# Attention of the later batches in 13 stretches of TensorE's time instead of 15, and a new written order of the other engines

## The chip, the cores and the metric

The kernel runs on one core of a Trainium2 chip. The metric is the time of one execution on the device in microseconds (us), the median of three runs. The core's engines run side by side, each through its own queue of instructions in a fixed order: TensorE (PE in the profile) multiplies, VectorE (DVE), ScalarE (ACT) and GpSimd (POOL) do everything else, and SyncE (SP) issues the transfers between memory and the on-chip buffer.

## What is computed

Chunked window attention over 4 batches of 8 heads, 768 positions and 64 columns, and behind it a mixture of 4 experts with 1024 hidden columns, in which every expert sees every token:

```python
# attention, for each chunk of 32 positions (window: 16 before, 8 after, and 8 memory keys)
scores = scale * q_c @ k_full.T
a = softmax(scores)
out[chunk] = a @ v_full
# experts, x = the attention's output as (3072, 512)
p = domain_probs / domain_probs.sum(-1)
for e in range(4):
    h = relu(x @ w1[e])           # (512, 1024)
    out += p[:, e:e+1] * (h @ w2[e])   # (1024, 512)
```

All of it is fp32. The large products are done in pairs of a rounded high part and the remainder (`_hi`, `_lo`), three matmuls for one, and by a scheme of seven block products instead of eight.

## The kernel before

**Stages.** The attention of one batch is cut into 8 units of 96 positions, 32 units in all. The first 60 us do batch 0's attention and its first expert. Then MID (n = 1 to 3, about 62 to 298 us) does the other experts of batch 0; it also makes the combinations of weights that the seven products need and stores them in memory. FIN (n = 4 to 15, about 298 us to the end) does batches 1 to 3, four experts each, with the weights streamed back in.

**Stretches.** The attention of the later units (8 to 31) is done between products of TensorE, in *stretches*: `window_of_two(us, vs)` puts the score matmuls of the units `us` (line 736) and the mixing matmuls, weights by values, of the units `vs` (line 758) onto TensorE one after the other. The softmax of the units scored in one stretch (a maximum on VectorE, the exponentials on ScalarE, a division and the transposes on VectorE) is done while TensorE goes on with the experts, and its result is mixed in the next stretch. The table `BY_TWO` says which units each stretch scores and mixes; its key is the step n and a place in it ("m" after the second pair of hidden columns, "A" after the last pair, "B" near the end). There are 15 stretches. The queries and keys of a unit are loaded ahead of its scores (`want_qk`) into one of a few places: a tile of their own (`qk_t`, in FIN for every second unit `qk_u`), or, in MID, a spare half of `xr` for the units in `SPARE`.

**The seven products.** In a step with pair p, the products of activations with the combined weights (line 999) come in the order one, two, six, five, seven of the pair and four and three of the pair before. Each leaves a result in `a_ps` or `moe_ps`, a few banks in turn, which ScalarE copies out (line 603) or VectorE adds up (line 621); then a relu (line 605), the multiplication with the routing weight (line 1101, `weigh`, or line 622 on GpSimd), a cast to the high part (`A_hi`, line 603) and the subtraction that leaves the remainder (`A_lo`, line 621 on VectorE or 622 on GpSimd). `Sa` and `Sb` are sums of such parts, `us` the steps of these sums. In MID the same engines also make the weights: `raw`, `s_t` and `raw_pair` are fp32 weights and their sums, `w` the parts for TensorE.

**What sets the order.** A list of operations is made in the order of the code; TensorE's own order follows it. For the other engines a written table, `MID_ORDER` or `FIN_ORDER`, names every operation by its number in base 36; an apostrophe means that it runs on the other engine that can do it (VectorE or GpSimd, ScalarE or VectorE). `follow` issues them in that order, and each engine then runs its queue strictly in that order, waiting for what its next instruction reads.

Of the kernel before, what the change touches and what calls it, by code (L numbers as in the profile page):

```python
# [18 lines left out]
P = 128  # L19
B, H, S, D = 4, 8, 768, 64  # L20
# [44 lines left out]
5k 67 5h 5p 7i 8u 5i 7p 6b 5m 7j 5s 6t 48 5q 5n 5u 8y 5r 5t 49' 7k 5o 7m 5w 5v 60 6e 7n 6m 4e 5x 6w 8v 61 6n 5y 6y 6f'
9m 62 7q 6x 7o 7t 4f 72 6v 5z 6s 8z 6u 7w 75 73 63 83 7u 77 81 6z 76 74 70 90 79 82 78 7x 7d 7v 7r a0 71 86 7s' 89 7z
91 7e 92 7y 7f 8w 8b 88 8a 7a 87 4a 84 8f 7b 9o 8c 9n 8i 7c 8d 8x 8g 7g 8k 4g a2 8j 80 8m 4h 96 8l 85 8h 99 4i 8q 94
4c 4j c9 ae 4b 4k 9e af 8r 4l ag 8s 4d ah 4m 9p ai 8n 9s aj 9q 4n 8o 8e 9u ak 9t 8p an 9v al 9r' am ar ao cb 8t ap ca
au at aq 9w cn 9f 97' as 9x 9a bx 9y a1 98' ax by 9b 9j 9c ay 9z bz 93 9d' 9h 95 c0 c1 cg cd' 9g c2 cl az ce c3 9i ch
# [1783 lines left out]
```

## Time and profile before

| | us |
|---|---|
| median of three runs | 1020.97 (1020.47 to 1021.89) |
| the profiled execution | 1021.78 |
| its span, first to last instruction | 1020.0 |
| TensorE busy in the span | 1011.6 (99%) |
| VectorE, GpSimd, ScalarE busy | 789.2 (77%), 544.5 (53%), 518.6 (51%) |

The granted clock of TensorE is 0.998 of full over the span. Read the table with the wait lists in mind: an engine that is 77% busy over the whole span can still be the one for which TensorE waits at one place.

### The profile page before, as it was taken

To read this page: it belongs to the slowest core of one execution; us is meant where nothing else is said; L and a number is where in the kernel's file an instruction comes from. 1 tells how busy PE (TensorE), PEld (TensorE's weight loads), DVE (VectorE), ACT (ScalarE), POOL (GpSimd) and SP (SyncE) were. 2 spreads that over 40 slices of the span, in tenths; PEclk is the share of its full clock that TensorE was granted. 3 is DMA by queue.
4 is the path that set the end of the run, shared out by engine and by line. 5 is a ranking of instruction groups with operands and counts; after the bars stand their busy time and mean duration, and the time that the engine had idled before them with its cause. 6 is when DMAs were issued, how large, how long until landed. Compare 5 with 4: busy or idle time off the path is not lost.

```text
span 1020.0 us, 20660 instructions
## 1 busy us (share of the span) xinstructions
PE 1011.6 (99%) x7566; PEld 975.3 (96%) x7566; DVE 789.2 (77%) x1245; ACT 518.6 (51%) x1415; POOL 544.5 (53%) x478
## 2 busy tenths in 40 slices
PE   8999999999999999999999999999999999999998
PEld 6898989989899999999999999999999999999998
DVE  5685987988969869797899759678697756849385
ACT  3756755747546465445655554453544535343241
POOL 4654733555559454586465714354276655527263
PEclk9999999999999999999999999999999999999999
DMA  8869989979789899899998987888778887878784
GB/s 274 293 210 363 362 324 390 382 286 382 282 288 354 292 377 312 301 367 313 353 291 280 287 269 252 287 267 276 236 253 277 293 263 257 271 246 278 248 257 146
DMA packets 184644, 299.28 MB, mean 293 GB/s; under 512 B 11904, under 2 KB 126176, under 8 KB 184544
## 3 DMA queue, kind: packets, MB, share of 16 engines
q1 hardware_dynamic: 184544, 297.97, 85.4%
q8 instruction: 60, 0.98, 0.4%
q14 instruction: 40, 0.33, 0.1%
HBM read 228.66 MB, written 69.26 MB: 292 GB/s over the span
## 4 chain that ended last, share of the span: by engine, by line
PE 98%; DVE 1%; issue 0%; ACT 0%; POOL 0%; DVEq 0%; POOLq 0%
PE a_ps L999 24%; PE a_ps L1289 20%; PE moe_ps L999 18%; PE moe_ps L1289 15%; PE moe_ps L978 13%; PE moe_ps L931 3%; PE s_ps L736 1%; PE x_ps L758 1%; PE moe_ps L758 1%; PE x_ps L1385 1%; PE att_ps L531 0%; DVE u L1101 0%; PE att_ps L1520 0%; PE att_ps L1476 0%; PE x_ps L1565 0%
## 5 line engine op out<-in xcount | busy, mean ns | idle before, releaser
L978 PE MATMUL moe_ps<-w,h_hi 128*128 128x512 f32 x384 | 119.4, 392 | 0.0
L603 ACT CAST A_hi<-u 128x384 fp32r<-128x384 f32 x144 | 72.8, 515 | 59.0 <-DVE u L1101 42.0
L603 ACT COPY u<-a_ps 128x384 f32<-128x384 f32 x120 | 57.2, 476 | 87.2 <-PE a_ps L999 86.8
L622 POOL TENSOR_TENSOR A_lo<-u,A_hi 128x384 fp32r<-128x384 f32 x47 | 53.1, 1133 | 83.5 <-ACT A_hi L603 83.5
L621 DVE TENSOR_TENSOR u<-moe_ps,u 128x384 f32<-128x384 f32 x120 | 66.1, 551 | 40.4 <-PE moe_ps L999 28.2
L999 PE MATMUL a_ps<-xc_hi,w 128*128 128x384 f32 x432 | 92.3, 334 | 0.0
L621 DVE TENSOR_TENSOR A_lo<-u,A_hi 128x384 fp32r<-128x384 f32 x97 | 84.5, 879 | 9.7 <-ACT A_hi L603 9.2
L978 PEld LDWEIGHTS moe_ps<-w,h_hi 128*128 128x128 f32 x384 | 71.3, 188 | 15.0
L622 POOL TENSOR_TENSOR u<-u,routes 128x384 f32<-128x384 f32 x43 | 45.3, 1056 | 75.4 <-ACT u L605 75.3
L1289 PE MATMUL a_ps<-A_hi,w 128*128 128x384 f32 x320 | 81.6, 335 | 0.1
L999 PEld LDWEIGHTS a_ps<-xc_hi,w 128*128 128x128 f32 x432 | 76.5, 188 | 0.5
L978 PE MATMUL moe_ps<-w,h_lo 128*128 128x512 f32 x192 | 75.0, 390 | 0.0
L621 DVE TENSOR_TENSOR acc<-a_ps,acc 128x384 f32<-128x384 f32 x78 | 42.9, 550 | 37.5 <-PE a_ps L1289 36.9
L1101 DVE SCALAR_TENSOR_TENSOR u<-u,routes 128x384 f32<-128x384 f32 x72 | 64.9, 911 | 0.2
L622 POOL TENSOR_TENSOR raw<-raw 128x256 f32<-128x256 f32 x41 | 37.2, 908 | 51.1 <-DVE raw L621 34.8
L621 DVE TENSOR_TENSOR u<-a_ps,u 128x384 f32<-128x384 f32 x60 | 33.1, 552 | 32.6 <-PE a_ps L999 27.3
L1289 PEld LDWEIGHTS a_ps<-A_hi,w 128*128 128x128 f32 x320 | 57.6, 188 | 0.8 <-DVE u L1101 0.6
L605 ACT ACTIVATE u<-u 128x384 f32<-128x384 f32 x72 | 37.9, 527 | 39.1 <-DVE u L621 38.6
L693 ACT ACTIVATE s_pair<-s_ps,mx_two 96x64 f32<-96x64 f32 x192 | 57.4, 322 | 0.3
L622 POOL TENSOR_TENSOR us<-u,us 128x384 f32<-128x384 f32 x33 | 41.3, 1252 | 26.1 <-DVE us L621 25.6
L999 PE MATMUL a_ps<-xc_lo,w 128*128 128x384 f32 x216 | 54.9, 334 | 0.0
L1289 PE MATMUL a_ps<-A_lo,w 128*128 128x384 f32 x160 | 53.5, 334 | 0.0
(254 smaller groups left out, 3068.8 us busy)
## 6 DMA issues: line engine op xcount, KB each, us to landing
w<-k SPq DMA_DIRECT2D x126, 512.0 KB, 4.6
w<-w SPq DMA_DIRECT2D x96, 512.0 KB, 5.5
w<-t SPq DMA_DIRECT2D x84, 512.0 KB, 6.0
k<-w SPq DMA_DIRECT2D x48, 512.0 KB, 5.9
raw<-in_w_dram SPq DMA_DIRECT2D x62, 256.0 KB, 5.2
w<-k SPq DMA_DIRECT2D x38, 256.0 KB, 4.5
raw_pair<-in_w_dram SPq DMA_DIRECT2D x32, 256.0 KB, 5.4
t<-t_hi SPq DMA_DIRECT2D x32, 256.0 KB, 5.6
```

What stands on the lines that cost most here:

```text
L603: nc.scalar.copy(out(), x())
L605: nc.scalar.activation(out(), x(), func)
L621: ("DVE", t_dve(cols), lambda: nc.vector.tensor_tensor(out=out(), in0=x(), in1=y(), op=op)),
L622: ("POOL", t_pool(cols), lambda: nc.gpsimd.tensor_tensor(out=out(), in0=x(), in1=y(), op=op)),
L693: now["plan"].add("ACT", t_act(KW) + 0.147, lambda i=i, h=h, j=j, g=g: nc.scalar.activation(whole()[:, i * H + h, :], at()[0:UQ, j, i, g, ...
L736: nc.tensor.matmul(at()[c * CH:(c + 1) * CH, j, i, g, :], lhsT=x[rows, g * UQ + c * CH:g * UQ + (c + 1) * CH], rhs=x[rows, k0:k0 + KW], st ...
L758: nc.tensor.matmul(out[j * D:(j + 1) * D, g, :], lhsT=late_st[w]["v"].ap[:, h * D:(h + 1) * D], rhs=late_st[w]["aT"][:, j * NPAIR + g, :], ...
L931: nc.tensor.matmul(ps.ap[:, lo:hi], lhsT=a[:, c * P:(c + 1) * P], rhs=x[:, c, lo:hi], start=(i == 0), stop=(i == len(steps) - 1),)
L978: nc.tensor.matmul(self.ps.ap, lhsT=h.ap[:, self.rows], rhs=w.ap[:, part, :], start=(i == 0 and k == 0), stop=(i == NF - 1 and k == 2),)
L999: nc.tensor.matmul(ps.ap[:, 0:SG], lhsT=a()[:, c * P:(c + 1) * P], rhs=y[:, k0 + c, :], start=(first and i == 0), stop=(i == len(steps) - ...
L1101: dve(lambda: nc.vector.scalar_tensor_tensor(out=u.ap, in0=x(), scalar=0.0, in1=r.ap, op0=ALU.max, op1=ALU.mult), SG, [r], [u] + keys, two ...
L1289: nc.tensor.matmul(ps.ap[:, 0:SG], lhsT=w_ap[:, y, rows], rhs=x.ap, start=(begins and k == 0 and i == 0), stop=(k == NP2 - 1 and i == 2), ...
```

## The change

Two stretches go: the one of step 3 in the middle of it ("m": scores of unit 15, mix of unit 14) and the one of step 7 ("m": scores of 23, mix of 21 and 22). Their units are put into the neighbouring stretches, which now score two units and mix two each. Unit 15's queries and keys are loaded into the spare half of `xr`, and those of unit 17, which would need a second tile, into a tile of `raw_pair` (the pool of the raw weight pairs, two places), after the last pair of step 3. No matmul is added or taken away; beside the stretches TensorE's order differs in four matmuls alone, the high part of the first product of pair (4, 0), which stand earlier, near the end of MID. Both tables of order are written anew; the diff shows the first line of one of them only. The lines of the functions move down by one to four (603 becomes 604, 621 and 622 become 622 and 623, 736 becomes 739, 1101 becomes 1105).

```diff
 MID_ORDER = """
-2 0 1q 1r 1 4 3 24 3n 3o 1s 5 1d x 1e 1i 8 1t 6 7 1k 1f y 1w b 1l 9 1y 1g 1u 11 a 2r 1h e 10 c d 1m 1v 15 h 1x f 1p t
+1r 0 2 1q 1 4 3 24 3n 3o 1s 5 1d x 1e 1i 8 1t 6 7 1k 1f y 1w b 1l 9 1y 1g 1u 11 a 2r 1m e 10 c d 1h z 15 h 1x f 1p t
...
 BY_TWO = {
-    (0, "B"): ((8, 9), ()), (1, "A"): ((10, 11), (8, 9)), (2, "A"): ((12, 13), (10, 11)), (2, "B"): ((14,), (12, 13)),
-    (3, "m"): ((15,), (14,)), (3, "A"): ((16,), (15,)),
-    (4, "A"): ((17, 18), (16,)), (5, "A"): ((19, 20), (17, 18)), (6, "A"): ((21, 22), (19, 20)),
-    (7, "m"): ((23,), (21, 22)), (7, "A"): ((24, 25), (23,)), (8, "B"): ((26, 27), (24, 25)),
+    (0, "B"): ((8, 9), ()), (1, "A"): ((10, 11), (8, 9)), (2, "A"): ((12, 13), (10, 11)), (2, "B"): ((14, 15), (12, 13)),
+    (3, "A"): ((16, 17), (14, 15)),
+    (4, "A"): ((18, 19), (16, 17)), (5, "A"): ((20, 21), (18, 19)), (6, "A"): ((22, 23), (20, 21)),
+    (7, "A"): ((24, 25), (22, 23)), (8, "B"): ((26, 27), (24, 25)),
     (9, "B"): ((28, 29), (26, 27)), (10, "B"): ((30, 31), (28, 29)), (11, "A"): ((), (30, 31)),
 }
-SPARE = (9, 11, 13)
+SPARE = (9, 11, 13, 15)
+LAST_RAW = (17,)
...
+        elif u in LAST_RAW:
+            t = new(lambda: late["sb"], [P, 2 * DM], "raw_pair", 2, parts=4)
...
-                        want_qk(u)
+                        if u not in LAST_RAW:
+                            want_qk(u)
...
+        for u in LAST_RAW if n == E - 1 else ():
+            want_qk(u)
         combine_some(COMBINED_A[n])
```

**VectorE at the end of n = 2.** The softmax of units 12 and 13, before: from the last steps ahead of the division (line 621, `s_pair`) to the transposes (lines 708 and 717), whose result `turn` the next stretch mixes.

```order
L699 TENSOR_SCALAR sm_two<-sm_two 96x16
L700 RECIPROCAL sm_two<-sm_two 96x16
L621 TENSOR_TENSOR raw<-raw 128x256
L621 TENSOR_TENSOR s_pair<-s_pair,sm_two 96x1024
L951 SCALAR_TENSOR_TENSOR acc<-moe_ps,pr,acc 128x512
L708 STREAM_TRANSPOSE turn<-s_pair 32x16x32
L717 STREAM_TRANSPOSE turn<-s_pair 32x8x32
L708 STREAM_TRANSPOSE turn<-s_pair 32x16x32
L717 STREAM_TRANSPOSE turn<-s_pair 32x8x32
L708 STREAM_TRANSPOSE turn<-s_pair 32x16x32
L717 STREAM_TRANSPOSE turn<-s_pair 32x8x32
L708 STREAM_TRANSPOSE turn<-s_pair 32x16x32
```

After, from the reciprocal of the same softmax; `w` are parts of weights, `h_lo` the remainder of an activation.

```order
L703 RECIPROCAL sm_two<-sm_two 96x16
L622 TENSOR_TENSOR s_pair<-s_pair,sm_two 96x1024
L622 TENSOR_TENSOR w_2876<-raw_pair,w_2876 128x512
L921 SCALAR_TENSOR_TENSOR h_lo<-u_2528,h_hi 128x384
L622 TENSOR_TENSOR w_2765<-s_t,w_2765 128x256
L955 SCALAR_TENSOR_TENSOR acc<-moe_ps,pr,acc 128x512
L720 STREAM_TRANSPOSE turn<-s_pair 32x8x32 x3
L955 SCALAR_TENSOR_TENSOR acc<-moe_ps,pr,acc 128x512
L711 STREAM_TRANSPOSE turn<-s_pair 32x16x32 x2
L720 STREAM_TRANSPOSE turn<-s_pair 32x8x32 x3
L622 TENSOR_TENSOR w_2930<-raw_pair,w_2930 128x256
L711 STREAM_TRANSPOSE turn<-s_pair 32x16x32 x2
```

Between the division and the first transpose stood one addition to `acc`; now three subtractions with both inputs in the buffer and an addition stand there, and one more subtraction (`w_2930`) among the transposes.

**VectorE after the stretch of n = 4**, before: the maximum of the scores (line 686) comes after the sums and remainders of the pair.

```order
L621 TENSOR_TENSOR Sa_lo<-us_4118,Sa_hi 128x384
L1101 SCALAR_TENSOR_TENSOR u_4151<-u_4151,routes 128x384
L621 TENSOR_TENSOR u_4028<-u_4028,us_4139 128x384
L621 TENSOR_TENSOR A_lo<-u_4151,A_hi 128x384
L621 TENSOR_TENSOR u_4270<-moe_ps,u_4270 128x384
L621 TENSOR_TENSOR Sa_lo<-us_4264,Sa_hi 128x384
L1101 SCALAR_TENSOR_TENSOR u_4295<-a_ps,routes 128x384
L1101 SCALAR_TENSOR_TENSOR u_4270<-u_4270,routes 128x384
L686 TENSOR_REDUCE mx_two<-s_ps 96x2x2x4
L621 TENSOR_TENSOR A_lo<-u_4270,A_hi 128x384
L621 TENSOR_TENSOR A_lo<-u_4295,A_hi 128x384
```

After: from the first step behind GpSimd's routing of `u_4045` on.

```order
L622 TENSOR_TENSOR us_4262<-u_4087,u_4045 128x384
L622 TENSOR_TENSOR u_4166<-a_ps,u_4166 128x384
L622 TENSOR_TENSOR A_lo<-u_3949,A_hi 128x384
L689 TENSOR_REDUCE mx_two<-s_ps 96x2x2x4
L622 TENSOR_TENSOR A_lo<-u_4110,A_hi 128x384
L622 TENSOR_TENSOR us_4295<-u_4020,us_4262 128x384
L1105 SCALAR_TENSOR_TENSOR u_4166<-u_4166,routes 128x384
L622 TENSOR_TENSOR u_4279<-moe_ps,u_4279 128x384
L1105 SCALAR_TENSOR_TENSOR u_4279<-u_4279,routes 128x384
L622 TENSOR_TENSOR A_lo<-u_4123,A_hi 128x384
L1105 SCALAR_TENSOR_TENSOR u_4330<-a_ps,routes 128x384
```

The step `us` moved here from GpSimd, and the maximum (now line 689) stands ahead of the additions that read `moe_ps` and of the multiplications.

**VectorE after the stretch of n = 5**, before: the maximum, then an addition from the products.

```order
L1101 SCALAR_TENSOR_TENSOR u_4920<-u_4920,routes 128x384
L621 TENSOR_TENSOR Sb_lo<-us_4896,Sb_hi 128x384
L621 TENSOR_TENSOR A_lo<-u_4834,A_hi 128x384
L686 TENSOR_REDUCE mx_two<-s_ps 96x2x2x4
L621 TENSOR_TENSOR u_5041<-moe_ps,u_5041 128x384
L621 TENSOR_TENSOR raw<-raw,t_hi 128x512
L1101 SCALAR_TENSOR_TENSOR u_5081<-a_ps,routes 128x384
```

After: the maximum first, and three remainders and the multiplication of `u_4958` behind it.

```order
L689 TENSOR_REDUCE mx_two<-s_ps 96x2x2x4
L622 TENSOR_TENSOR Sa_lo<-us_4870,Sa_hi 128x384
L622 TENSOR_TENSOR A_lo<-u_4865,A_hi 128x384
L622 TENSOR_TENSOR A_lo<-u_4884,A_hi 128x384
L1105 SCALAR_TENSOR_TENSOR u_4958<-u_4958,routes 128x384
L622 TENSOR_TENSOR raw<-raw 128x256
L1105 SCALAR_TENSOR_TENSOR u_5119<-a_ps,routes 128x384
```

**ScalarE at the same place**, before: the copies out of the stretch's results (`xr`) and of the first product (`u_5041<-a_ps`), and only then the scaling of the maximum.

```order
L603 COPY xr<-x_ps 128x4x96
L603 COPY xr<-moe_ps 128x4x96
L603 CAST A_hi<-u_4869 128x384
L603 COPY u_5041<-a_ps 128x384
L605 ACTIVATE u_4820<-u_4820 128x384
L603 CAST A_hi<-u_4985 128x384
L607 ACTIVATE mx_two<-mx_two 96x16
```

After: the scaling and four exponentials, the cast of `u_4958`, and only then the copies, the last of them that of the first products.

```order
L608 ACTIVATE mx_two<-mx_two 96x16
L696 ACTIVATE s_pair,sm_two<-s_ps,mx_two 96x64 x4
L604 CAST A_hi<-u_4958 128x384
L604 COPY u_5097<-a_ps 128x384
L604 COPY xr<-x_ps 128x4x96
L604 COPY xr<-moe_ps 128x4x96
L604 COPY u_5121<-a_ps 128x384
```

The copy out of `a_ps` now stands behind the cast of `u_4958`, which reads what VectorE multiplies three remainders after the maximum.

## Rows read from the trace of the kernel before

**Rows 1.** The page, part 4: the chain that ended last, by engine
```profile
PE 98%; DVE 1%; issue 0%; ACT 0%; POOL 0%; DVEq 0%; POOLq 0%
```

**Rows 2.** Windows: a stretch, its length, busy us (instructions) of each engine, clock
```profile
62.00:1018.00 956.00, 954.51 (x6673) 926.06 (x6671) 750.47 (x1170) 485.82 (x1303) 511.37 (x440) 1.00 0.86 294
```

**Rows 3.** TensorE's timeline around n = 3's middle stretch: start, us, line, out<-in
```profile
239.63 0.51 PE L999 MATMUL moe_ps<-xb_lo,w 128*128 128x384 f32 x2
239.98 0.85 PE L999 MATMUL a_ps<-xc_hi,w 128*128 128x384 f32 x4
240.67 0.51 PE L999 MATMUL a_ps<-xc_lo,w 128*128 128x384 f32 x2
243.40 0.52 PE L999 MATMUL a_ps<-xa_lo,w 128*128 128x384 f32 x2
```

**Rows 4.** TensorE's timeline around the stretches of n = 4 and n = 5
```profile
313.23 0.51 PE L999 MATMUL a_ps<-xc_lo,w 128*128 128x384 f32 x2
314.82 0.88 PE L758 MATMUL x_ps<-turn,v_t 128*64 128x96 f32 x16
316.44 0.51 PE L999 MATMUL a_ps<-xa_lo,w 128*128 128x384 f32 x2
...
373.64 0.51 PE L999 MATMUL a_ps<-xc_lo,w 128*128 128x384 f32 x2
375.23 0.88 PE L758 MATMUL x_ps<-turn,v_t 128*64 128x96 f32 x16
377.50 0.51 PE L999 MATMUL a_ps<-xa_lo,w 128*128 128x384 f32 x2
```

**Rows 5.** Timeline of VectorE and GpSimd, three A_lo beside GpSimd, three Sa_lo alone
```profile
310.31 3.49 DVE L621 TENSOR_TENSOR A_lo<-u,A_hi 128x384 fp32r<-128x384 f32 x3
...
312.06 1.33 POOL L622 TENSOR_TENSOR u<-u,u 128x384 f32<-128x384 f32 x1
...
399.06 1.48 DVE L621 TENSOR_TENSOR Sa_lo<-u,Sa_hi 128x384 fp32r<-128x384 f32 x3
```

**Rows 6.** Timeline of VectorE and TensorE at the end of n = 2
```profile
204.13 0.36 DVE L621 TENSOR_TENSOR raw<-raw 128x256 f32<-128x256 f32 x1
204.41 1.76 DVE L621 TENSOR_TENSOR s_pair<-s_pair,sm_two 96x1024 f32<-96x1024 f32 x1
206.09 0.74 DVE L951 SCALAR_TENSOR_TENSOR acc<-moe_ps,pr,acc 128x512 f32<-128x512 f32 x1
206.75 0.69 DVE L708 STREAM_TRANSPOSE turn<-s_pair 32x512 f32<-32x512 f32 x1
207.46 0.44 DVE L717 STREAM_TRANSPOSE turn<-s_pair 32x256 f32<-32x256 f32 x1
213.18 0.86 DVE L621 TENSOR_TENSOR raw<-raw,t_hi 128x512 fp32r<-128x512 f32 x1
...
215.90 0.88 PE L758 MATMUL x_ps<-turn,v_t 128*64 128x96 f32 x16
```

**Rows 7.** Timeline of GpSimd, VectorE and TensorE after the stretch of n = 4
```profile
314.90 1.16 POOL L622 TENSOR_TENSOR u<-u,routes 128x384 f32<-128x384 f32 x1 [0.24 <-ACT u L605]
...
317.41 1.37 DVE L621 TENSOR_TENSOR A_lo<-u,A_hi 128x384 fp32r<-128x384 f32 x1
321.01 1.21 DVE L686 TENSOR_REDUCE mx_two<-s_ps 96x16 f32<-96x1024 f32 x1
...
321.98 0.68 PE L999 MATMUL a_ps<-xc_hi,w 128*128 128x384 f32 x3
```

**Rows 8.** Timeline of ScalarE and TensorE after the stretch of n = 5
```profile
378.05 0.48 ACT L603 COPY u<-a_ps 128x384 f32<-128x384 f32 x1 [0.34 <-PE a_ps L999]
378.85 0.50 ACT L603 CAST A_hi<-u 128x384 fp32r<-128x384 f32 x1
...
379.93 0.68 PE L999 MATMUL a_ps<-xc_hi,w 128*128 128x384 f32 x3
```

**Rows 9.** The tile qk_t: from a load's issue to its landing
```profile
DMA to landing us min/median/max: 4.3/6.2/8.7
```

More of the change, by code (lines that the diff above doesn't have):

```diff
@@ L65 @@
[L65 to L69, printed above, removed]
@@ L201 @@
[L201 to L203 removed]
+7 p 8 r' q s' 4 5y 5 9 f g v t w' 6 1k a x h i j 13 b k 15 y 2l 14 16 c d 2 l m' 1b n 17 1f 1g u' o z 1h 1j 1c 18' 1o
+1 5z 19 1a 1l 10 1p 1q 1z 1i 20 60 25 27 1d 1e 0 26 2c 3 1r 28 2d 21 1v 22' 1s' 1u' 1n 2m 1m 2g 2o 2e 2h 12 23 2i 1x
@@ new lines @@
+y4 z6 z1 uq z9 yc za z7 uh zb z0 z8 uw zc zd z2 zh ux ze zi zj zf v2 zk y6 zg v3 zn zo v4 zp y8 zr zq v5 ye zv y9' zs
+zl zw v6 zm zx xf zy uy ya xg yg' 103 v0 v7 104 zz v8 uz yb' yh 10b v9 10h 105 10c yd 10d 10f 10e 10k va 10g yf 100
+10m 10l vb zt 10p 10o 10n 106 zu yi 107 10w 10q 108 10r 10y v1 10s 10x 10i 109 114 10z 11e 10t' 10j 110 118 10a 10u
+111 115 11a 10v 116 119 117 112 11c 11f 11b 113 11r 11g 11d 11h 11y 11t 11s 11i' 11u 120 11z 11j 125 121 11v 11n 12f
+122 129 11l 11w 126 123 11x 12b 127 11k 12a 124 12d 12c 12g 11o' 11p 12s 128 12e 11m 12y 12u 12t 12h 130 12v 12z 12i
@@ new lines @@
+1mp 1nh 1mi 1mj 1nj 1mk 1ni 1ml 1nk 1mm 1mo 1nl 1ms 1nn 1nm 1mu 1mv 1nq 1mw 1np 1no 1mr 1nr 1mx 1mn 1ns 1mt 1nt 1my
+1nv 1mz' 1nu 1nw 1nx 1nz 1ny 1o2 1o1 1o0 1n4 1o3 1n0 1o4 1n5 1n6 1o5 1n1 1o9 1o6 1oa 1n7 1n2 1oh 1n8 1ob 1on 1oi 1n3
+1n9 1oj 1na 1ol 1oc 1ok 1nb 1od 1op 1oo 1om 1nc 1or 1oe' 1oq 1nd 1of 1ou 1ot 1og' 1os 1p1 1ow 1ov 1ox 1p3 1p2 1oy' 1oz
+1p9 1p4 1pj 1p0' 1p5 1pd 1pa 1p6' 1pb 1pf 1pe 1pc' 1p7 1ph 1p8 1pg 1pk 1pw 1pl 1pi 1pm 1q3 1py 1px 1pn' 1pz 1q5 1q4
+1po' 1q0' 1ps 1pp 1qa 1pq' 1q1 1qk 1qe 1pu 1pr 1q6 1qb 1qg 1qf 1pt 1qc 1q7 1qi 1qd' 1pv 1qh 1ql 1q8 1qx 1qj 1qm 1q9
@@ new lines @@
+1r3 1qn 1qy 1qz 1qo 1q2 1r6 1qp 1r4 1r0 1r5 1r8 1r7 1qr 1qq' 1qt 1tv 1rd 1rn 1tx 1r9 1qs 1rh 1re 1qv 1ra 1rf 1ty' 1rj
+1ri 1qu 1rb 1r1 1rl 1ro 1rk 1qw' 1rz 1rc 1rm 1s5 1s0 1s6 1s1 1rg 1s7 1rp 1s8 1s2 1sa 1rq 1s3 1s9 1rr 1se 1sb 1r2 1sc
+1vv 1sq 1rt 1rv 1sg 1sf 1sr 1tz 1sd 1ss 1rw' 1su 1st 1sh 1sx 1sv 1rs 1sy 1sw 1vw 1sz 1si' 1t0 1rx 1ru 1tw 1t3 1sm 1t4
+1ry' 1t5 1t7 1t6 1sn 1tb 1t8 1tc 1sj 1t1 1td 1sk' 1te 1t2 1u1' 1so 1tg 1s4 1th 1tn 1ti 1tp 1tk 1tj 1tr 1ud 1u6 1sp
+1ts' 1tl 1ue 1tq 1tt 1uf 1ug 1to 1ui 1tu 1uj 1up 1uh 1uk 1tf 1ur 1uq' 1um 1ul 1tm 1ut 1ux 1sl' 1us' 1un 1uy 1uo 1uv
@@ new lines @@
+22n 22m 22l 22o 22p 22q 22u 22r 22v 232 22w 238 233 22x 234 22y 236 235 22z 23a 239 237 230 23c 23b 231 23f 23e 23d
+23m 23h 23g 23i 23o 23n 23j 23u 23p 244 23k 23q 23l' 23y 23v 23w 23r 240 23z 23x 23s 242 245 241 23t 24h 246 243 247
+24o 24j 24i 248 24k 24q 24p 24l 24v 24r 255 249 24m 24s 24z 24d 24b 24w 24t 251 24a' 24x 250 24u 24f 24c 253 256 24e
+252 25i 254 257 24n 25o 258 25j 25k 259' 25q 25p 24y 25a 25l 25v 265 25e 25b 25z 25r 25m 25w 25c 25s 261 25g 260 25x
+25d 263 262 266 25y' 26h 25f 264 25t 267 26n 25u 26i 26o 25h' 26j 26p 268 26q 26s 24g 269' 26w 26r 26d 26b 26t 26a'
@@ L204 @@
+2ml' 2mo 2mp 2ms 2mq 2mt 2mr 2mu 2mv 2my 2mw 2mz 2mx 2n0 2n1 2n4 2n2 2n5 2n3 2n6 2n7 2na 2n8 2nb 2n9 2nc 2nd 2ng 2ne
+2nh 2nf 2ni 2nj 2nk 2nl
 """
@@ L227 @@
 LOCK = 0.14
+FLIGHT = 850e3
 LATENCY = {"PE": 0.055, "ACT": 0.035, "DVE": 0.035, "POOL": 0.08, "SP": 0.12}
```

252 lines of the change are left out of this document (116 added, 136 removed).

## The prediction, made before the changed kernel ran

> **What bounds the kernel now.** I read the chain of work that ended last first: the reader sees that 98% of it is TensorE [rows 1]. Then the windows: from 62 us, where batch 0's attention is over, to 1018 us TensorE is busy 954.51 of 956.00 us at the full clock [rows 2]. So the other engines cost next to nothing now, and all waits that a better order could still take away there sum to 1.49 us. The time can move in two ways only: TensorE gets less to do, or it begins to wait. Last I read TensorE's timeline where the stretches lie, and the timelines of VectorE, GpSimd and ScalarE beside them, for how late each result is and by how much TensorE could have had it later.
>
> **What goes: two stretches' fixed cost.** In a row of products the four matmuls of a high part take .69 us from start to start (239.98 to 240.67) and the two of a low part .35 (239.63 to 239.98) [rows 3]. What a stretch adds is the time from the end of the low part ahead of it to the start of the high part behind it. One score unit and one mix: 243.40 - .69 - (240.67 + .35) = 1.69 us [rows 3]. Two and one: 316.44 - .69 - (313.23 + .35) = 2.17; two and two: 377.50 - .69 - (373.64 + .35) = 2.82 [rows 4]. The differences give .48 us for a score unit and .65 for a mix unit, so that 1.69 - .48 - .65 = .56 us is left for each stretch, whatever is in it. The change moves all units and drops none; two stretches fewer are worth 2 x .56 = 1.1 us. That is the whole of the certain gain. If every wait after 62 us went too, it would be 1.1 + 1.5 = 2.6.
>
> **What it may cost: results that come later.** Merged stretches mean softmaxes of two units where there were softmaxes of one, so VectorE's work comes in larger lumps, and the new order moves thirteen two-input operations from GpSimd to VectorE over MID and FIN, at places where GpSimd has work queued as well. What that costs I take from one pair of rows: three subtractions `A_lo` in a row took 3.49 us on VectorE while GpSimd ran sums of its own (one of them 1.33 us long), and three of the same shape took 1.48 with GpSimd idle [rows 5]. So an operation with two inputs in the buffer costs .47 us alone and .67 more beside GpSimd ((3.49 - 1.48)/3); one A_lo alone shows 1.37, which is .82 over the .55 of an undisturbed one [rows 7] (1.48 - 2 x .47). Additions that read a bank of the products and transposes I charge no delay.
>
> The Trainium skill, "SBUF — State Buffer", section "SBUF: two separate sides", says that a VectorE instruction with two buffer inputs and a GpSimd instruction that reads the buffer take an exclusive lock on a shared port pair, for the whole instruction of whoever starts first. The rows agree in direction; by that rule alone a VectorE operation could wait out a whole 1.33 us GpSimd operation, while the pair of rows shows about half of it.
>
> *Stretch of n = 5.* S = 375.23 is the start of its mix before, unchanged in size after (two and two) [rows 4]. The fourth product behind it starts at 379.93, S + 4.70 [rows 8], and needs a bank that ScalarE has copied out. Before, that copy ran at 378.05 [rows 8], free of the softmax. After, it stands on ScalarE behind the scaled maximum, four exponentials and the cast of an activation which VectorE multiplies only after the maximum and three remainders. Alone: .2 from S to the maximum, 1.21 for it [rows 7], 1.48 for three remainders [rows 5], .55 for the multiplication (as one undisturbed A_lo), then .50 for the cast and .48 for the copy [rows 8]: S + 4.42, in time by .3. But GpSimd's queue there has a remainder, a multiplication and a sum, all with inputs ready. With 3.49 instead of 1.48 it is S + 6.43, a stall of 1.7; if the multiplication is held up as well, 2.4. Bounds 0 to 2.4; I take 2.0, since the place resembles the 3.49 row most.
>
> *Stretch of n = 4.* It grows from two and one to two and two. S = 314.82 [rows 4]. The step `us` moved from GpSimd to VectorE can't start before GpSimd's multiplication ends, at 314.90 + 1.16 = 316.06 = S + 1.24 [rows 7]. From there VectorE's queue has ten operations of .47 and the maximum, 1.21, up to the multiplication out of `a_ps`: S + 7.15; then ScalarE's cast .50 and the copy .48 [rows 8]: S + 8.13. The seventh product behind wants the bank at 321.98 - 314.82 = 7.16 [rows 7], and .65 later for the added mix unit: S + 7.81. Alone that is a stall of .3. Before, the maximum came at 321.01 [rows 7], behind those additions; now it and the step stand ahead of them. Seven of the ten have both inputs in the buffer. One held up by GpSimd gives 1.0, two 1.6, three 2.3. I take 1.3, between one and two, since GpSimd's queue there partly waits for transfers and casts. Bounds 0 to 2.3.
>
> *End of n = 2.* The mix of units 12 and 13 starts at 215.90 [rows 6], and .48 later with a second score unit: 216.38. Before, VectorE was through the division at 206.09 and went to the transposes after one addition, .66. After, the `raw` step (.28) ahead of the division is gone; since GpSimd holds the division up here I leave its end at 206.09. Behind it now stand a subtraction of 512 columns (.86), `h_lo` (.47), one of 256 (.28), the addition (.66), then four transposes of .71 and six of .44, another addition (.66) and another 256 (.28): 206.09 + .86 + .47 + .28 + .66 + 5.48 + .66 + .28 = 214.78 [rows 6], 1.6 to spare. Three of these can be held up beside the 512, whose row may hold a wait already: + 3 x .67 gives 216.8, + 3 x .82 gives 217.2, and 218.1 if the 512 waits .82 more. So the stall is .4, .9 or 1.7; GpSimd has more than four operations of two inputs queued in this part. I take 1.0, near the middle, bounds 0 to 1.7.
>
> *Elsewhere.* The other merged stretches (n = 3, 6, 7) and the moved operations: the covered time seems enough at each; I take .5 us in all, between 0 and the 1.5 us that all waits now amount to [rows 2]. The earlier four matmuls of pair (4, 0) are the same work on TensorE and cost nothing if their operand is ready, as xa is at that point. Unit 17's load now goes into a raw pair's place when that is free, later than a `qk_t` would be; loads of this kind land 4.3 to 8.7 us after issue [rows 9]. I take nothing, but up to 2 us if a slow one meets its scores.
>
> Sum: -1.1 + 1.0 + 1.3 + 2.0 + .5 = +3.7 us. The profiled execution took 1021.78 (span 1020.0), so it would be 1025.5; the median of the three runs shown, 1020.97, is .8 under it, so I forecast 1024.7.
>
> **Rivals.**
> 1. *VectorE keeps up*, since the operations that I called held up fall between GpSimd's. For it: alone, every chain but one arrives in time. Against: three in a row did stall each other [rows 5]. Time: 1020.97 - 1.1 = 1019.9, no change that can be told. This is the one that ends on the other side.
> 2. *Only n = 5 stalls*, where one copy stands behind a whole softmax start, and the two others are covered. 1020.97 - 1.1 + 2.0 = 1021.9, also no change.
> 3. *All waits go*: the new order also clears the 1.49 us. 1020.97 - 2.6 = 1018.4, faster. Against: the places above.
> 4. *Unit 17 comes late*: the main sum and 2 us: 1026.7. For it: the load waits for a place in another pool. Against: it has the tail of the pair ahead of it.
> 5. *Whole operations are waited out*: each held-up VectorE operation waits 1.33 instead of .67. Eight of them (three at n = 5, two at n = 4, three at n = 2), .66 each: 1024.7 + 5.3 = 1030.0. Against: the 3.49 us for three [rows 5]. This is what the page's lock would give at its worst.
>
> **How the numbers follow.** A measurement of this kernel can tell about 0.2%, 2.0 us: faster is under 1018.9, slower over 1023.0. Main forecast .60, of which I put .04 under 1023.0 (all three places at the small end); rival 1 .13, rival 2 .16, rival 3 .03, rival 4 .05, rival 5 .03. So faster .03; no change .04 + .13 + .16 = .33; slower .56 + .05 + .03 = .64. The likeliest case's own range is 1022.8 to 1026.8 (its terms lie between 0 and their upper ends, not all at one end). The range for 8 in 10 leaves out rival 3, rival 5 and part of rivals 1 and 4: 1020.3 to 1026.8.
>
> **What would show it.** TensorE's waits after 62 us, 1.5 us now, should be five to six. The largest wait of TensorE should stand at the fourth product behind the stretch of n = 5, with ScalarE's copy of `a_ps` as what released it, about 2 us; the next at the seventh product behind that of n = 4; and the mix at the end of n = 2 should wait for VectorE's transposes. In front of the first VectorE should show A_lo of 1 us and more with GpSimd busy beside. The stretches should sum 1.1 us less of TensorE's time. The forecast is wrong if TensorE is busy as fully as before after 62 us (then rival 1), if the transposes at the end of n = 2 end before their mix (that term), or if the scores of unit 17 wait for their load (rival 4).

## The result, and the profile after

The changed kernel is slower: 1027.87 us, median of 6 runs (1026.23 to 1029.04), against 1020.78 (1020.15 to 1022.37, 6 runs) of the kernel before on the same chip. The ratio is 1.0065 [1.0052, 1.0078], so 5.3 to 8.0 us. The forecast was 1024.7 with a range up to 1026.8: the direction was right, the time lies outside. The profiled execution took 1026.45 (span 1024.7); it is 1.4 us under the median of its kernel, while that of before is .8 to 1.0 over its own.

The page of after, part 1 and part 4 (the chain that ended last), and its window from 62 us to the last products:

```profile
PE 1012.7 (99%) x7566; PEld 974.0 (95%) x7566; DVE 788.4 (77%) x1242; ACT 515.7 (50%) x1413; POOL 523.2 (51%) x465
...
PE 71%; DVE 4%; issue 3%; POOL 1%; ACT 1%; DMA 0%; SPq 0%; POOLq 0%; DVEq 0%; ACTq 0%
```

```profile
62.00:1022.00 960.00, 954.69 (x6668) 924.43 (x6666) 747.53 (x1166) 482.60 (x1300) 487.97 (x425) 1.00 0.87 293
```

Where the chain was TensorE to 98% [rows 1], it now shows 71%. The shares sum to about 80%, because the chain is followed back to 197 us only; of the 828 us from there TensorE has about 88%. The rest ran back through VectorE, GpSimd and ScalarE, because TensorE waited for them. TensorE stands idle 960.00 - 954.69 = 5.31 us in the stretch, against 956.00 - 954.51 = 1.49 before [rows 2]. What it waited for, from the wait list of after (engine and line, what released it, us in total, times, longest):

```profile
PE a_ps L1003 <- ACT u L604: 2.8, 2, 1.9
PE x_ps L762 <- DVE turn L711: 1.3, 1, 1.3
PE att_ps L1524 <- issue: 1.2, 1, 1.2
PE att_ps L532 <- issue: 1.2, 2, 0.8
PE x_ps L1389 <- POOL idle L502: 1.0, 1, 1.0
PE moe_ps L982 <- DVE h_lo L921: 0.3, 1, 0.3
PE a_ps L1003 <- DVE u L622: 0.2, 1, 0.2
```

The first two rows are the three places that the prediction named; `att_ps` and `x_ps L1389` belong to the first stage, and before had such waits too.

**The place at n = 5.** Timelines of after: VectorE, GpSimd, ScalarE and TensorE from the maximum to the fourth product.

```profile
379.75 1.21 DVE L689 TENSOR_REDUCE mx_two<-s_ps 96x16 f32<-96x1024 f32 x1
380.88 0.70 DVE L622 TENSOR_TENSOR Sa_lo<-us,Sa_hi 128x384 fp32r<-128x384 f32 x1
381.50 2.65 DVE L622 TENSOR_TENSOR A_lo<-u,A_hi 128x384 fp32r<-128x384 f32 x2
384.08 1.35 DVE L1105 SCALAR_TENSOR_TENSOR u<-u,routes 128x384 f32<-128x384 f32 x1
...
379.89 1.28 POOL L623 TENSOR_TENSOR Sb_lo<-us,Sb_hi 128x384 fp32r<-128x384 f32 x1 [2.91 <-ACT Sb_hi L604]
381.12 1.33 POOL L623 TENSOR_TENSOR A_lo<-u,A_hi 128x384 fp32r<-128x384 f32 x1
382.42 1.32 POOL L623 TENSOR_TENSOR u<-u,routes 128x384 f32<-128x384 f32 x1
383.82 1.20 POOL L623 TENSOR_TENSOR us<-u,u 128x384 f32<-128x384 f32 x1
...
385.46 0.51 ACT L604 CAST A_hi<-u 128x384 fp32r<-128x384 f32 x1 [2.94 <-DVE u L1105]
385.88 0.47 ACT L604 COPY u<-a_ps 128x384 f32<-128x384 f32 x1
...
386.41 0.96 PE L1003 MATMUL a_ps<-xc_hi,w 128*128 128x384 f32 x4 [1.90 <-ACT u L604]
```

Read it as a ladder. Each VectorE operation runs beside one of GpSimd, and a pair takes 1.30 us, where VectorE alone needs .47 to .55. So the multiplication ends late (2.3 us, by quiet_gpsimd below), ScalarE's cast waits 2.94 us for it, the copy stands behind the cast, and the product waits 1.90. In before the copy ran ahead of the softmax and nothing waited [rows 8].

**Where the time went.** The same matmul stands in both traces, and its later start shows what was lost up to it (us, counted from a matmul at 61 us):

| place | predicted | measured |
|---|---|---|
| stretches and units | -1.1 | -1.14 |
| end of n = 2, mix waits for transposes | +1.0 | +1.38 |
| stretch of n = 3 and what follows it | in "elsewhere" | +1.56 |
| behind n = 4 | +1.3 | +1.50 |
| behind n = 5 | +2.0 | +2.19 |
| all else | +.5 | +.18 |
| sum from 61 us on | +3.7 | +5.67 |

In these two profiles the changed kernel reaches 61 us .96 us earlier than before, so the whole executions differ by 4.67 us only.

The n = 3 part is spread thin: .51 in the stretch, then .25, .33 and .47 up to 262 us, nearly all below what the wait list prints. It shows in the timeline of TensorE in after, where four matmuls of a high part take .97 instead of .85:

```profile
240.56 0.51 PE L1003 MATMUL moe_ps<-xb_lo,w 128*128 128x384 f32 x2
240.94 0.97 PE L1003 MATMUL a_ps<-xc_hi,w 128*128 128x384 f32 x4
241.75 0.51 PE L1003 MATMUL a_ps<-xc_lo,w 128*128 128x384 f32 x2
```

Two matmuls to the next start are .35 [rows 3]; .38 here means .03 of waiting, and .81 instead of .69 to the row behind means .12 more until TensorE is in step again. The wait of 1.90 us above has the same tenth on top (.96 for its first four matmuls).

About half of this part comes and goes. In the profiles of quiet_gpsimd, copies_first, three_given_n2 and load_behind (experiments, below), none of which edits anything at n = 3, TensorE loses about .75 us less up to 246 us. VectorE's remainder `h_lo` and GpSimd's operation in front of it, in after and then in copies_first:

```profile
239.76 1.44 DVE L921 SCALAR_TENSOR_TENSOR h_lo<-u,h_hi 128x384 fp32r<-128x384 f32 x1
239.04 1.74 POOL L623 TENSOR_TENSOR w<-raw_pair,w 128x512 fp32r<-128x512 f32 x1
...
241.37 0.55 DVE L921 SCALAR_TENSOR_TENSOR h_lo<-u,h_hi 128x384 fp32r<-128x384 f32 x1
239.61 1.28 POOL L623 TENSOR_TENSOR w<-raw_pair,w 128x512 fp32r<-128x512 f32 x1
```

In the first the two overlap, in the second GpSimd is through before VectorE begins. That isn't all of it: in after_again and fill_wait `h_lo` takes 1.43 and 1.49 as well, and .2 and .6 us less are lost.

### The profile page after: what moved, and what is told of

It is laid out like the page before. It is cut to its first block, busy times and chain, and to the rows that moved or that the text cites. A ratio compares the mean times of both kernels' runs of the same rounds, so it can differ in the third digit from the quotient of the medians.

```text
span 1024.7 us, 20602 instructions
## 1 busy us (share of the span) xinstructions
PE 1012.7 (99%) x7566; PEld 974.0 (95%) x7566; DVE 788.4 (77%) x1242; ACT 515.7 (50%) x1413; POOL 523.2 (51%) x465
## 4 chain that ended last, share of the span: by engine, by line
PE 71%; DVE 4%; issue 3%; POOL 1%; ACT 1%; DMA 0%; SPq 0%; POOLq 0%; DVEq 0%; ACTq 0%
PE a_ps L1293 19%; PE a_ps L1003 19%; PE moe_ps L1293 15%; PE moe_ps L1003 14%; PE moe_ps L982 3%; DVE h_lo L921 1%; PE s_ps L739 1%; DVE u L1105 1%; DVE A_lo L622 1%; PE x_ps L762 1%; POOL s_t L623 1%; DMA v_t<-in_v_dram 0%; PE moe_ps L762 0%; DVE u L622 0%; DVE w L622 0%
## 5 line engine op out<-in xcount | busy, mean ns | idle before, releaser
L623 POOL TENSOR_TENSOR A_lo<-u,A_hi 128x384 fp32r<-128x384 f32 x44 | 49.1, 1119 | 90.0 <-ACT A_hi L604 90.0
L623 POOL TENSOR_TENSOR u<-u,routes 128x384 f32<-128x384 f32 x41 | 42.8, 1046 | 72.3 <-ACT u L606 72.1
L1105 DVE SCALAR_TENSOR_TENSOR u<-u,routes 128x384 f32<-128x384 f32 x72 | 60.8, 853 | 0.3
L623 POOL TENSOR_TENSOR raw<-raw 128x256 f32<-128x256 f32 x36 | 32.6, 906 | 53.4 <-DVE raw L622 37.4
L606 ACT ACTIVATE u<-u 128x384 f32<-128x384 f32 x72 | 37.9, 526 | 38.0 <-DVE u L622 37.6
L622 DVE TENSOR_TENSOR acc<-moe_ps,acc 128x384 f32<-128x384 f32 x66 | 36.2, 551 | 22.3 <-PE moe_ps L1293 21.9
```

What stands on the lines that cost most here:

```text
L606: nc.scalar.activation(out(), x(), func)
L622: ("DVE", t_dve(cols), lambda: nc.vector.tensor_tensor(out=out(), in0=x(), in1=y(), op=op)),
L623: ("POOL", t_pool(cols), lambda: nc.gpsimd.tensor_tensor(out=out(), in0=x(), in1=y(), op=op)),
L1105: dve(lambda: nc.vector.scalar_tensor_tensor(out=u.ap, in0=x(), scalar=0.0, in1=r.ap, op0=ALU.max, op1=ALU.mult), SG, [r], [u] + keys, two ...
```

## The experiments

The time "from 61 us" below is that of the profile between the same two matmuls, as its difference from before; each kernel has one profile. Ratios are to runs of before on the same chip.

| kernel | median us (n) | ratio | from 61 us |
|---|---|---|---|
| quiet_gpsimd | 1024.13 (6) | 1.0035 [1.0023, 1.0047] | +2.71 |
| copies_first | 1025.66 (5) | 1.0042 [1.0030, 1.0055] | +3.33 |
| three_mended | 1025.56 (5) | 1.0034 [1.0021, 1.0048] | +2.26 |
| no_waits | 1020.27 (11) | .9990 [.9981, .9999] | -1.73 |
| nine_given | 1022.78 (9) | 1.0022 [1.0012, 1.0031] | +.36 |
| three_given_n2 | 1025.28 (1) | | +3.74 |
| three_given_n3 | 1025.40 (1) | | +4.16 |
| after_again | 1028.53 (5) | 1.0068 [1.0056, 1.0080] | +6.66 |
| load_behind | 1026.64 (6) | 1.0049 [1.0037, 1.0061] | +6.27 |
| load_ahead | 1022.25 (11) | 1.0010 [1.0002, 1.0019] | +.11 |
| no_waits_behind | 1020.46 (11) | .9989 [.9981, .9998] | -1.60 |
| fill_wait | 1026.61 (6) | 1.0046 [1.0032, 1.0060] | +4.86 |

**quiet_gpsimd: GpSimd kept out of n = 5.** Three operations with two inputs (`au`, `bc`, `bo`) go to VectorE, one of them behind the multiplication:

```diff
-... da au' as bm ... cg bz c3 ... dl bc' ... bo dn
+... da as bm ... cg bz au c3 ... dl bc ... bo' dn
```

> The changed kernel with one edit behind the stretch of n = 5: three of GpSimd's operations with two buffer inputs (Sb_lo, A_lo, us) are given to VectorE, the first of them behind the multiplication of u_4958, so that GpSimd has next to nothing while VectorE does its three remainders and that multiplication. ScalarE's order is untouched: the copy of a_ps stays behind the softmax and the cast. Theory 1 (GpSimd lengthens VectorE's operations, and that alone makes the copy late): the three remainders and the multiplication take about .55 us each, TensorE's wait at the fourth product behind the stretch falls from 1.90 us to under .3, and the time from 1027.9 to about 1025.9. Rival (the copy's place behind maximum, exponentials and cast makes it late whatever GpSimd does): the wait stays at 1.5 us or more and the time at 1027.9.

Timeline of VectorE, ScalarE and TensorE in this kernel:

```profile
380.61 0.85 DVE L622 TENSOR_TENSOR Sa_lo<-us,Sa_hi 128x384 fp32r<-128x384 f32 x1
381.39 1.01 DVE L622 TENSOR_TENSOR A_lo<-u,A_hi 128x384 fp32r<-128x384 f32 x2
382.33 0.54 DVE L1105 SCALAR_TENSOR_TENSOR u<-u,routes 128x384 f32<-128x384 f32 x1
...
383.33 0.47 ACT L604 COPY u<-a_ps 128x384 f32<-128x384 f32 x1
...
384.08 0.85 PE L1003 MATMUL a_ps<-xc_hi,w 128*128 128x384 f32 x4
```

The two A_lo take 1.01 instead of 2.65, the multiplication .54 instead of 1.35, the copy starts 3.85 us after the maximum's start at 379.48 instead of 6.13 (385.88 - 379.75), and the product doesn't wait. VectorE has more work here and is done sooner. ScalarE's order is as in the changed kernel, so it is shown that GpSimd beside it makes VectorE late, and that the wait goes with it. From 61 us on 2.96 us are gone: 2.19 here, the rest at n = 3, in the part that comes and goes.

**copies_first: the copy ahead of the cast.** GpSimd stays; ScalarE's copies no longer stand behind the cast that waits for VectorE (`c0` behind `c9`).

```diff
-bz c3 c0 d9 dj ex' c8 c9 c6
+bz c3 d9 dj ex' c8 c9 c0 c6
```

> The changed kernel with ScalarE's cast of u_4958 moved behind the copies of a_ps and of both mixes at n = 5; VectorE's and GpSimd's order untouched, so VectorE's remainders stay as long as they are (2.65 us for two, 1.35 for the multiplication). If the wait is that copy's and nothing else: TensorE's wait of 1.90 us at the fourth product goes, the cast comes .9 us later and its products wait up to .5 us at about 393 us; time about 1026.3. If the place behind was only one of several that come late together, a wait of over 1 us shows up at the next product instead, and the time stays over 1027.

VectorE's pair stays slow, and yet the fourth product runs through:

```profile
382.29 2.66 DVE L622 TENSOR_TENSOR A_lo<-u,A_hi 128x384 fp32r<-128x384 f32 x2
384.87 1.36 DVE L1105 SCALAR_TENSOR_TENSOR u<-u,routes 128x384 f32<-128x384 f32 x1
...
385.11 0.85 PE L1003 MATMUL a_ps<-xc_hi,w 128*128 128x384 f32 x4
```

Of the 2.19 us, .73 comes back at 391 and 394 us, where the same late activation is used (`[0.22 <-DVE u L1105]` and smaller ones). So the stall needs both: a slow VectorE, and a copy queued behind its result.

**three_mended: one order mended at each of the three places.** As copies_first, and one or two numbers moved at the end of n = 2 and behind n = 4 (`o0`, `ny` later in MID, `4n` later in FIN).

```diff
-kx lx ky ny i5 ... m7 o0 mk ... l1 l2 o3
+kx lx ky i5 ... m7 mk ... l1 l2 o0 ny o3
-2x' 4n 2w' 4r 4t 4q 57
+2x' 2w' 4r 4t 4q 4n 57
```

> The changed kernel with three small moves: at the end of n = 2 the subtractions w_2876 and w_2930 go behind the last transpose; behind the stretch of n = 4 ScalarE's copy of a_ps goes ahead of the cast of u_4330; at n = 5 the copies go ahead of the cast of u_4958. If these three places carry the loss, TensorE's waits of 1.30, .92 and 1.90 us go, about 1.0 us of smaller ones comes or stays, and the time is 1027.9 - 3.4 = 1024.5. If the loss was spread or comes from elsewhere (transfers, unit 17's load, the clock), it stays over 1026.5.

From 61 us on it takes 3.4 us less than the changed kernel; .23 is left at n = 2 (beside the added score unit), .84 at n = 4, .92 at n = 5, and n = 3 keeps its loss. By the ratios it is 3.2 us less, by the medians alone, which stand beside different runs of before, 2.3; 1024.5 was expected. Its five runs spread from 1022.8 to 1026.3, and in the profile the first 61 us were 2.3 us longer than in before (more on that below).

**three_given_n2 and three_given_n3.** At the end of n = 2 (`m2`, `jn`, `ji`), and around n = 3 (`t8`, `s4`, `rs`), three GpSimd operations go to VectorE, with no change of order.

```diff
-je ji lf ... lo jl me jn' jp ... mg m2' mh
+je ji' lf ... lo jl me jn jp ... mg m2 mh
```
```diff
-pv rs' nv ... u1 s4' rt ... s2 t8 sb
+pv rs nv ... u1 s4 rt ... s2 t8' sb
```

> Only the three of the end of n = 2 (two steps of raw, one part of a weight) from GpSimd to VectorE: TensorE's wait of 1.30 us ahead of the mix at 217 us goes by over 1 us, nothing else changes. If the larger softmax alone makes the mix late, the wait stays at 1.3 or grows.

> Only the three of n = 3 (two parts of weights, one sum s_t) from GpSimd to VectorE: the small waits at 242, 244, 250 and 262 us, 1.5 us with their restarts, fall to under .4; the places n = 2, 4 and 5 keep theirs. If those small waits come from transfers or from the merged stretch at the end of n = 3, they stay.

In the first, the wait of the mix at the end of n = 2 falls; row of TensorE:

```profile
216.49 0.88 PE L762 MATMUL x_ps<-turn,v_t 128*64 128x96 f32 x16 [0.22 <-DVE turn L711]
```

1.30 became .22. Of the 1.93 us that it gains from 61 us on, 1.08 are this; most of the rest are the .75 at n = 3 that come and go, so "nothing else changes" did not hold. In the second, the four steps of n = 3 (1.56 us) are zero. TensorE runs through there:

```profile
240.96 0.51 PE L1003 MATMUL moe_ps<-xb_lo,w 128*128 128x384 f32 x2
241.31 0.85 PE L1003 MATMUL a_ps<-xc_hi,w 128*128 128x384 f32 x4
242.00 0.51 PE L1003 MATMUL a_ps<-xc_lo,w 128*128 128x384 f32 x2
```

So the loss at n = 2 has the same cause as that at n = 5. At n = 3 it is shown for the steps at 250 and 262 us, .80 us, which of the profiles above only this one lacks; the .75 before them are absent from four kernels without the edit, and a single profile can't tell what the edit did there. Both kernels were run once.

**nine_given: nine GpSimd operations to VectorE, no number moved.** Those six and three more (`bn`, `bq`, `2t`) in FIN.

```diff
-bc' dg dk bn db
+bc' dg dk bn' db
```

> The changed kernel with nine of GpSimd's 468 two-input operations given to VectorE at their old places in the order, three each at the end of n = 2, in n = 3, and behind the stretches of n = 4 and n = 5; no operation is moved. Theory (the two engines hold each other up, VectorE's late results are those beside GpSimd): VectorE has about 4 us more to do and TensorE still waits less: 4 to 5 of the 5.7 us that the changed kernel lost after 61 us come back, time 1027.9 - 4.5 = 1023.4. Rival (VectorE has too much to do in larger lumps, the stretches themselves are too long for it): the nine make VectorE later, the waits grow, time 1028 or more.

The page, part 1:

```profile
PE 1010.6 (99%) x7566; PEld 973.5 (95%) x7566; DVE 785.3 (77%) x1251; ACT 515.6 (51%) x1413; POOL 508.8 (50%) x456
```

VectorE runs nine instructions more than in the changed kernel and is busy 3.1 us less (788.4 to 785.3). 5.3 of the 5.67 us are gone: 1.09 at n = 2, 1.55 at n = 3 (with the .75 that come and go), .70 of the 1.50 at n = 4, 1.6 of the 2.19 at n = 5, and smaller ones. Six of its runs lie at 1022.1 to 1022.8, three at 1024.9 to 1026.1; what the three had is not seen in the one profile.

**no_waits: the 13 stretches with an order in which nothing waits.** At least 251 numbers of the two tables moved (the text below says about 140) and 14 marks changed, chosen by the durations of the trace with VectorE and GpSimd taking turns at 1.30 us a pair. Around the copy of n = 5:

```diff
-as bm b0 b1 cb bi cd ce bk ch b8 c7 dp df cg bz c3 c0 d9 dj ex' c8 c9 c6 dl
+az da bm b0 b1 cb bi cd as bk b8 c7 dp df cg bb bz c3 c0 d9 dj ex' c8 ch ce c9 c6 dl
```

> The changed kernel's 13 stretches with about 140 of the operations of VectorE, ScalarE and GpSimd moved and 14 changed between VectorE and GpSimd, so that no result comes late by the durations of the traces; TensorE's and SyncE's order untouched. If the waits after 62 us and the restarts behind them (a second matmul .11 us late after each) are the whole loss, 5 to 6 us go: 1022 us. If waits cost more than their length in the timed runs (a lower granted clock after them in some), it comes to the time before less the two stretches: about 1019.5, under the kernel before.

Its wait list, here the five longest, has the first stage alone, but for one row of .4 (`a_ps L1004`):

```profile
PE att_ps L1525 <- issue: 2.2, 1, 2.2
PE x_ps L1390 <- POOL idle L503: 1.0, 1, 1.0
PE att_ps L533 <- issue: 0.7, 1, 0.7
PE moe_ps L983 <- ACT h_hi L607: 0.7, 1, 0.7
PE a_ps L1004 <- DVE u L623: 0.4, 1, 0.4
```

From 61 us on it is 1.73 us faster than before: the 1.14 of the stretches and .6 elsewhere, where before had waits of its own. By its ratio it is .1 to 1.9 us faster than before; that is near the limit of what can be told, and the second measurement (no_waits_behind) gives the same. The time lies between the two that were expected (1022 and 1019.5). The 13 stretches themselves, then, cost nothing; the new order of the other engines, and which of them runs what, did.

**What the sum leaves: 1.4 us.** The trace from 61 us on has 5.67 of the 7.1 us between the medians. Two theories were tried. The first looks at the first stage. MID_ORDER now begins with a load of `raw`, 256 KB, which gets into SP's queue ahead of the last load of `spot`; after it TensorE waits at 41 to 45 us (above all .35 for `h_lo`), where before had no wait. The same four numbers were put the old way into the changed kernel and into no_waits, and the new way into the kernel before.

```diff
-1r 0 2 1q 1 4 3
+2 0 1q 1r 1 4 3
```

> The changed kernel itself, as the measure for load_behind on the same chip. Theories D and N alike: 1027 to 1028.5; by D, TensorE's drift against before between 36 and 48 us lies at 0.5 to 3 us in its profile again, by N it may be zero this time.

> The changed kernel with the first four numbers of MID_ORDER in the order of before (2 0 1q 1r for 1r 0 2 1q), so that the 256-KB load of raw that heads the second stage no longer stands ahead of the last load of spot in SP's queue. Theory D (that load takes the DMA engines from spot's, ScalarE's cast of spot comes late, and TensorE waits at 41 to 45 us): no idle time of TensorE between 36 and 48 us, the drift over that stretch against before falls from +1.00 us to under 0.2, the rest of the kernel from 61 us on stays at +5.7 us, and the median falls by 0.9 to 1.6 us, to 1026.3 to 1027.0. Theory N (the first 61 us differ from run to run by chance, and the 0.35-us wait at 43.55 us is part of that): the median stays within 0.5 us of the changed kernel's on the same chip.

> The kernel before with the first four numbers of MID_ORDER in the order of after (1r 0 2 1q), and nothing else. Theory D: TensorE, which had no idle time between 36 and 48 us, waits there 0.3 to 2 us for h_hi or h_lo behind ScalarE's cast of spot, and the median rises by 0.5 to 1.5 us over the kernel before. Theory N: the median stays within 0.4 us of the kernel before.

> The version no_waits with the first four numbers of MID_ORDER in the order of before. Theory D: its first 61 us lose the 0.66 and 0.35 us that TensorE waited at 42 and 45 us, and the median is 1018.7 to 1019.6, ratio 0.9975 to 0.9985 of the kernel before. Theory N: 1020.3 plus or minus 0.4, ratio 0.999.

The medians are for it twice (load_behind 1.9 us under after_again, load_ahead 1.0 over before) and against it once (no_waits_behind: no gain). The traces are against it. TensorE of no_waits_behind, with the load behind:

```profile
41.98 0.73 PE L983 MATMUL moe_ps<-w,h_hi 128*128 128x512 f32 x2 [0.35 <-ACT h_hi L607]
44.80 0.74 PE L983 MATMUL moe_ps<-w,h_hi 128*128 128x512 f32 x2 [0.35 <-DVE h_lo L922]
```

and load_ahead, with the load ahead, has no idle time there (window):

```profile
36.00:48.00 12.00, 12.00 (x65) 11.01 (x64) 9.36 (x18) 6.94 (x30) 9.32 (x10) 1.00 0.67 258
```

What decides is when TensorE gets there: in the nine profiles where it reaches 37.6 us at least 1.0 us earlier than in before, it loses 1.0 to 3.7 us up to 45 us; in those where it is later by .2 and more it loses none. So the mechanism falls, and whether the load's place costs anything stays open. That loads set the time there is likely, but not shown. From profile to profile the arrival at 61 us varies, from .96 us earlier to 2.30 later than in before.

The second theory came from the profiles of after_again and load_behind. Windows of after_again, behind the wait of 1.91 us at n = 5 (the column before the last two is the granted clock):

```profile
384.00:388.00 4.00, 2.09 (x12) 1.77 (x11) 3.81 (x6) 1.65 (x4) 1.77 (x2) 0.97 1.07 377
388.00:391.00 3.00, 3.00 (x11) 3.00 (x10) 0.93 (x2) 1.60 (x5) 0.19 (x1) 0.50 1.07 385
```

and TensorE's rows there:

```profile
387.24 1.22 PE L1003 MATMUL a_ps<-xc_hi,w 128*128 128x384 f32 x4 [1.91 <-ACT u L604]
388.26 0.84 PE L1003 MATMUL a_ps<-xc_lo,w 128*128 128x384 f32 x2
388.90 1.48 PE L1003 MATMUL moe_ps<-xc_hi,w 128*128 128x384 f32 x4
390.18 0.84 PE L1003 MATMUL moe_ps<-xc_lo,w 128*128 128x384 f32 x2
```

Four matmuls take 1.28 us to the next start instead of .69: .50 is the lower of TensorE's two clock levels, 1.2 GHz, and it came within .8 us after TensorE had begun again. The profile of the changed kernel, with the same wait, stayed at 1.00:

```profile
388.00:391.00 3.00, 3.00 (x19) 3.00 (x18) 1.64 (x3) 3.00 (x14) 1.56 (x2) 1.00 1.03 385
```

Among the five profiles with that wait, two have the slow passage; it costs 1.56 us. The Trainium skill, "TensorE: Matmul & The Clock Gate", section "Part 1: The HAM clock gate", says that "the default state is throttled, and activity releases the throttle"; the rows agree as to the direction, idle time first and the lower level behind it.

The single runs bear on this too, since each has its mean granted clock on record. Of the 17 runs of the changed order (after, after_again, load_behind) the eight with .996 or less take 1028.4 us on average, the nine others 1026.7. Of 64 runs of before only ten lie at .996 or less, and they take 1021.7 against 1021.4. So a low mean is more frequent in the changed order, and it goes with 1.6 us there and with .2 in before. It is no proof: in a run without a profile it isn't known where the clock was low, and the first stage alone can bring the mean down (the profile of fill_wait, below, has .995, with 1.00 behind n = 5). Four of the five runs of after_again are in the low group and two of the six of load_behind, so part of the gap between their medians needs no moved load.

**fill_wait: TensorE computes instead of waiting.** Ten useless matmuls stand ahead of the second product behind n = 5, in the bank that this product starts anew.

```diff
+        fill = 10 if now["products"] == 132 else 0
...
+            for i in range(fill):
+                a, y, c = steps[i % len(steps)]
+                nc.tensor.matmul(ps.ap[:, 0:SG], lhsT=a()[:, c * P:(c + 1) * P], rhs=y[:, k0 + c, :],
+                                 start=(i == 0), stop=False, skip_group_check=True)
```

> The changed kernel with ten more matmuls (10 x 0.173 = 1.73 us) ahead of the second product behind the stretch of n = 5, into the bank that this product then starts anew, so that TensorE computes instead of standing idle in its 1.9-us wait for ScalarE's copy. It leaves nothing out. Theory H (the granted clock falls to its lower level behind that idle time, in two of the three profiles of the changed order, and that costs 1.5 us each time; it is the part of the 7.1 us that the profile of the changed kernel, 1.4 us under its own median, didn't show): the granted clock stays at 1.00 from 380 to 400 us, TensorE's wait at the fourth product is under 0.4 us, the products behind it take 0.17 us a matmul, the runs lie between 1025.8 and 1027.2 and the median is 1026.3 to 1026.9, ratio 1.0048 to 1.0056, although the extra matmuls take nearly as long as the wait. Theory L (the low clock comes by chance, whatever TensorE did before): the runs spread from 1026 to 1029 with the median at 1027.9 to 1028.5, ratio 1.0065 to 1.007, as for the changed kernel.

(The "two of the three profiles" in this text are of after, after_again and load_behind; the two three_given kernels have the wait too, without the slow passage.) Row of TensorE and window:

```profile
386.95 0.96 PE L1010 MATMUL a_ps<-xc_hi,w 128*128 128x384 f32 x4 [0.20 <-ACT u L604]
```

```profile
388.00:391.00 3.00, 3.00 (x19) 3.00 (x18) 1.51 (x3) 2.71 (x10) 1.03 (x2) 1.00 1.05 386
```

The extra work cost 1.72 us and took 1.70 off the wait, so without the clock nothing should have moved; the median is 1.3 to 1.9 us under the two measurements of the changed kernel. But load_behind, which keeps the wait, has the same median (1026.64). Three of the six runs are outside what was expected (1028.59, and 1025.69 twice), the ratio is just under it, and .6 of the .8 us that this profile gains on that of after lie at 241 to 246 us, where nothing was edited. So fill_wait by itself settles little. Theory H is supported by it together with the clocks of the single runs; its share in the medians (about .6 us, if two runs in five have the passage) isn't settled.

## Why the prediction was wrong

- *The fixed cost of a stretch* was right: -1.14 against -1.1.
- *The mechanism* was right at each place named: VectorE beside GpSimd makes a late result and TensorE waits, at n = 4 and 5 for ScalarE's copy that stands behind it, at n = 2 for the transposes themselves. By moving GpSimd's operations it was taken away at n = 2 and n = 5, at n = 3 for .80 us, and at n = 4 by half (nine_given).
- *The three waits* were each somewhat larger (1.38, 1.50, 2.19 for 1.0, 1.3, 2.0; together .77). The price of .67 us for a held-up operation is a mean over three: the first `A_lo` of [rows 5] started with .5 us of GpSimd's operation left and took .84 to the next start, the other two 1.29. Where the two engines take turns from the start the pair takes 1.30, so a held-up operation costs about .8.
- *The step that failed* is the sum, in two places. The first is its term "*Elsewhere.* The other merged stretches (n = 3, 6, 7) and the moved operations: the covered time seems enough at each; I take .5 us in all". It measured 1.74, of which n = 3 alone cost 1.56, though .75 of that comes and goes. n = 3 lies in MID, where VectorE and GpSimd make the weights as well, and no chain was worked out for it. The 1.24 us of this term and the .77 above are the difference of 5.67 to 3.7.
- *The second* is what the sum put at nothing without a reason: what a wait costs TensorE beyond its length. That is a tenth of a us until it is in step again, and, behind the 1.9-us wait, in some runs 1.56 us at half clock. The range ended at 1026.8, with terms that were waits only. The profiled execution (1026.45) lies inside it, and so, just, does the average of the nine runs with the higher clock (1026.7); that of the eight with the lower one (1028.4) does not.
- *Rival 4* (unit 17's load) didn't come true: no wait at its scores. *Rival 5* had a price of 1.33 for a hold-up that costs .8; that the two engines wait for each other by turns fits it. Rivals 1 to 3 fall with the waits; rival 3's price for an order without waits, 2.6 us under before, was not reached: no_waits gained 1.73 from 61 us on.
- 1.4 us of the difference in the medians is not in the profile of after from 61 us on, and stays open. The low clock behind the wait is the likeliest part of it, argued from the clocks of the runs. The first 61 us can't be excluded; load_ahead (+1.0, four numbers changed) hints at the moved load there, but its profile is .86 us late at 25 us already, before that load goes out at 33.66, and no_waits_behind contradicts.

## What to carry to other kernels

When TensorE is busy 99%, the gain from merging pieces of its work is bounded by their fixed costs (here 1.1 us), while a new order of the other engines can lose several times that. Work out the chain for every place that changes, not only for the longest. Before moving an operation with two inputs from VectorE to GpSimd to relieve VectorE, see what stands beside it: with nine more taken back from GpSimd VectorE was busy 3.1 us less. And before crediting an edit with a gain, see in other profiles whether the place varies without it. And put on an engine's queue what TensorE waits for ahead of what waits for another engine.

## What the hardware showed that was not expected

- VectorE and GpSimd, both with two-input operations in the buffer, alternate at 1.30 us a pair, in ladders four long (379.89 to 385.02 us); GpSimd's operation alone takes 1.01 (before, at 377.79 us), VectorE's .47 to .55.
- A wait of .03 us of TensorE was followed by .12 more in the next matmuls, as was one of 1.90.
- A wait of 1.9 us was followed by the lower clock level in two of five profiles, at 1.56 us of cost. In three_mended the same follows a wait of 1.98 us at 43 us (granted clock .82 at 43 to 45 us, .55 at 45 to 48 us). In the first stage nearly every profile shows the lower level for a while, that of before too (.89 on average from 10 to 25 us).
